# One PSUM bank for two running states, a seventh rotating bank, reordered output sessions, an earlier gate for the second weights, and last stores by halves

## The chip, the cores and the metric

The kernel runs on one NeuronCore of a Trainium2 chip, in one launch. The metric is the device time in microseconds (us) of that core. TensorE is called PE here, its weight loads PEld, VectorE is DVE, ScalarE is ACT, GpSimd is POOL, and SyncE, which issues most DMAs, is SP.

## The reference

The program is a retention layer (attention with an exponential decay in place of a softmax) followed by a two-layer network. Cut to what matters:

```python
# q, k, v: 8 batches x 8 heads x 576 positions x 64, float32
scores = q @ k.T / 8                          # per batch and head
gamma  = 1 - 2 ** (-5 - arange(8))            # one decay per head
ret    = scores * where(i >= j, gamma ** (i - j), 0)
x      = (ret @ v)                            # rearranged to 4608 tokens x 512
h      = x @ w_in                             # 512 -> 2048
g      = h * cos(h)
out    = g @ w_out                            # 2048 -> 512
```

## The kernel before

**Retention.** The decay is folded into q and v by tables of weights (`qnat`, `natv`), so that only a mask of zeros and ones is left. Work goes by units: unit (b, g) with g = 0 or 1 is positions 256g to 256g+255 of batch b; units (0, 2) and (1, 2) hold the remaining 64 positions of four batches each. Each unit's 256 positions fall into two halves, s = 0 and 1. What a later query needs of all earlier halves is the sum of k-times-v products, the running *state*: 64x64 for each head, 128x256 numbers for a batch. The state grows in PSUM (`ST`, one bank for the even batch `ST[0]` and one for the odd, `ST[1]`), and `snap` (L631) has ACT copy it to SBUF after each half.

All these matmuls are 64x64: PE is used as four quadrants, the *lanes* (row half, column half), and `emit_lanes` (L540) interleaves the instructions of the lanes. A *session* is one such run of small matmuls. A scores session (L565) makes q-k products, which DVE multiplies with the mask into `pt` (L599). An output session (`outputs`, L637) has three batches:

- main: products of `pt` and v for both halves, and the state products whose row lane is the same half's;
- states (only where there are any, `late`): the states of (u, 1) in the row lanes s = 1 and of the next unit's first half in the row lanes s = 0;
- cross: state products that run in the other half's row lanes. They add to the same banks as main, and so wait for it, by a semaphore that PE raises itself.

Two states of different batches, in two row halves of PE, thus run side by side, each into its own bank. The first state matmul of a batch clears the bank with `start=True` (L623).

**The network.** For each block j of 512 tokens (9 blocks) `mlp1` (L727) makes 16 tiles of h, four matmuls each (L737); ACT takes the cosine (L745, as a sine of h + pi/2), DVE the product into `gt` (L748). The second layer of block 0 is plain (`plain2`, L767, matmuls L776). From block 1 on it is a Strassen-Winograd product (`wino2`, L805, matmuls L862): seven products P1 to P7 in place of eight, with sums of `gt` (DVE, L823 and L829) and of the weights (`wsums`, L787, DVE L802); ACT and DVE combine them into `os`, and SP stores (`store`, L753). Products with a common sum share a PSUM bank: A, Bb and C.

**PSUM.** A partition has eight banks. Two hold the states, six rotate (`bk`): every score, output, h tile and product takes one and returns it once ACT or DVE has read it.

**The order.** It is written by a planner at build time (`Graph.run`, L204): each piece of work is a task with an engine, an estimated duration, what it reads and writes, the rotating buffers it takes, and a priority. The planner places tasks one by one on five in-order queues. It has a simple model of PE's instruction supply: every 256 instructions (`count`) a task may have to wait until 3.0 us (`FETCH`) after the last request. Where the plan has a gap on PE longer than 0.4 us, early in the kernel, `emit` (L375) puts in filler matmuls on ones (`warm`, L398). Then the list is turned into instructions with semaphores (`Prog.emit`).

**Loads.** SP loads k, q and v of each unit (0.5 MB each); POOL casts k, weights q and v. POOL also issues the weights, with a conversion to bf16: four pieces of `win` (L717) and four of `wout` (L721). The issue of `wout` waits until v of unit (1, 1) has landed; the loads of unit (2, 0) wait for the second piece of `wout` (L940 to L943):

```python
gate = [(st["v", (1, 1)], 0)]
for x in range(4):
    self.load_w("wout", x, gate, 200 + x)
self.unit((2, 0), gate=[("wout", 1, 0)])
```

Of the kernel before, what the change touches and what calls it, by code (L numbers as in the profile page):

```python
# [6 lines left out]
ALU = mybir.AluOpType  # L7
# [10 lines left out]
NTB = TOK // TB  # L18
# [111 lines left out]
class Graph:  # L130
# [3 lines left out]
    AHEAD, FETCH = 2000, 3000  # L134
# [44 lines left out]

    def first(self, t):  # L180
# [23 lines left out]
    def run(self, dma_rate):  # L204
# [3 lines left out]
        left = [256, self.FETCH]  # L208
# [21 lines left out]
        def pick(e):  # L230
            cand = []
            for t in ready[e]:
# [4 lines left out]
                if e == "pe" and t.count > left[0]:  # L237
                    s = max(s, left[1] - t.dur * left[0] / t.count)
# [22 lines left out]
        while n < len(self.tasks):  # L261
# [10 lines left out]
            e = t.eng  # L272
            ready[e].remove(t)
# [5 lines left out]
            if e == "pe":  # L279
                if t.count > left[0]:  # L280
                    left[1] = s + t.dur * left[0] / t.count + self.FETCH
                    left[0] += 256
                left[0] -= t.count
# [9 lines left out]
            if t.dma is not None:  # L293
                dma_free = max(dma_free, s + (1700 if e == "pool" else 1150)) + t.dma
                done = dma_free + t.tail
# [18 lines left out]
class Kernel:  # L314
    POOLS = dict(bk=6, stgk=3, stgv=3, stgq=3, natk=3, natv=3, qnat=2, kt=3, qt=3, pt=4, sba=3, sbb=3, sbr=8, xt=2,
# [11 lines left out]
    def __init__(self, nc, es, q, k, v, w_in, w_out, out):  # L327
# [20 lines left out]
        self.ST = [nc.alloc_psum_tensor(f"st{i}", [128, 512], F32) for i in range(2)]  # L348
# [26 lines left out]
    def emit(self, order):  # L375
# [4 lines left out]
        for t in order:  # L380
            if t.eng == "pe":
                gap = t.start - warm
                if gap > 400 and self.wb.left:
                    self.warm(int((gap - 300) / 110 if not warm else 0.6 * (gap - 150) / 57))
# [126 lines left out]
    def tpe(self, src, off, rk, dst, wk, eng):  # L511
        bk = Buf("bk")

        def mm(e):
            tb = self.at(bk).ap().bitcast(BF16)
            for c in range(4):
# [5 lines left out]
                 alloc=() if self.first else (self.wb,), name="tpe", count=9)  # L522
# [17 lines left out]
    def emit_lanes(self, name, prio, phases, alloc=()):  # L540

        parts, t, n = [], 200, 0
        for lanes, reads, writes, after in phases:
# [7 lines left out]
            n += 2 * len(order) + 1  # L551
# [60 lines left out]
    def states(self, u, s, lanes, reads, writes):  # L612
        nk, nv = self.tiles[u]["natk"], self.tiles[u]["natv"]
        x = u[0] % 2
        for r in range(2):
            for c in range(4):
                for y in range(2):
                    i, o = 512 * y + (2 * c + r) * D, 512 * y + self.head(c, r) * D
                    lanes[s, r].append((64, self.mm(
                        lambda r=r, c=c: ap(self.ST[x], 512, 64 * r, 64, c * 64, [1, 64]),  # L620
                        lambda i=i: ap(self.at(nk), 1024, 64 * s, 64, i, [1, D]),
                        lambda o=o: ap(self.at(nv), 1024, 64 * s, 64, o, [1, D]),
                        start=u[1] == s == c == y == 0)))  # L623
        reads += [(t, y) for t in (nk, nv) for y in range(2)]
        writes.append(("st", x))
# [5 lines left out]
    def snap(self, u, s):  # L631
        b = self.sbd[u, s] = Buf("sba" if s == 0 else "sbr" if u[1] else "sbb")
        x = u[0] % 2
        self.copy("act", 280, lambda: self.at(b).ap(), lambda: ap(self.ST[x], 512, 0, 128, 0, [1, 256]),
                  [("st", x)], [(b,)], late=1000 if s == 0 else 3000)

    def outputs(self, u, prio, late):  # L637
# [5 lines left out]
        main, fill, cross = ({q: [] for q in self.LANES} for _ in range(3))  # L643
# [37 lines left out]

        for s in range(2):
# [3 lines left out]
        for s in range(2):  # L686
            for p in range(2):
                inter(s, p, 1 - s, cross)
# [5 lines left out]
        phases = [(main, reads, writes, [])]  # L694
        if late:
# [305 lines left out]
```

## Time and profile before

| | us |
|---|---|
| median of three runs | 302.74 (300.94, 302.74, 304.18) |
| the profiled execution | 301.62 |
| its span, first to last instruction | 299.9 |
| PE busy | 285.2 (95% of the span) |
| DVE busy | 213.0 (71%) |
| ACT busy | 169.7 (57%) |
| POOL busy | 101.4 (34%) |
| DMA, mean rate | 166 GB/s |

A PE that is called busy is not PE at its peak, since matmuls overlap and their ends are modelled. By line, the chain that ended last is 35% L737 (first layer) and 33% L862 (second layer), then 8% loads of q, 6% L563 (small matmuls), and 3% each for the two weights. Loads of q, k and v take a median of 6.9 to 7.0 us from issue to landing, the pieces of `win` 9.0 and of `wout` 10.0, a store 3.3.

In the lines of a timeline the columns are: start in us, length in us, engine, line, operation, what it writes and reads, how many; in brackets the idle time of the engine before it and what ended that. In lists of waits: who waited for whom, us in total, how often, the longest.

### The profile page before, as it was taken

The numbers are of one execution on the slowest core, as the hardware profiler recorded it, in microseconds if no ns is written. First come the engines' busy times: TensorE is split into PE (matmuls) and PEld (weight loads), VectorE is DVE, ScalarE is ACT, GpSimd is POOL, SyncE is SP. The second block draws the span as 40 slices with busy tenths as digits, with TensorE's granted clock in tenths as the row PEclk, the third lists the DMA queues.
The fourth block names the chain that finished last, engine by engine and source line by source line (L and its number), as shares of the span: only waits on it lengthen the run. The fifth ranks groups of instructions, "written<-read, shape, count | busy, mean of one in ns | idle before, by whom it ended". The sixth has DMA issues, their size and how long they took to land.

```text
span 299.9 us, 9086 instructions
## 1 busy us (share of the span) xinstructions
PE 285.2 (95%) x3809; PEld 202.7 (68%) x3815; DVE 213.0 (71%) x379; ACT 169.7 (57%) x315; POOL 101.4 (34%) x125
## 2 busy tenths in 40 slices
PE   6789888999999999999999999999999999999994
PEld 6667665666788876766676667666766666666683
DVE  2776495659985889697868686959777666667721
ACT  5369876556667565645655565466565555545420
POOL 3821960665825614825363515172100000000000
PEclk9999999999999999999999999999999999999999
DMA  7999789999999799997999986892103000300115
GB/s 199 252 203 274 202 129 236 280 200 299 207 251 297 151 194 281 214 227 210 229 280 232 244 188 94 194 236 53 24 2 140 2 2 2 140 2 0 70 73 140
DMA packets 101640, 49.87 MB, mean 166 GB/s; under 512 B 43488, under 2 KB 97248, under 8 KB 101600
## 3 DMA queue, kind: packets, MB, share of 16 engines
q1 hardware_dynamic: 97376, 45.10, 63.6%
q0 software_dynamic: 4224, 4.19, 8.8%
q8 instruction: 30, 0.49, 0.7%
q14 instruction: 10, 0.08, 0.1%
HBM read 36.70 MB, written 9.44 MB: 154 GB/s over the span
## 4 chain that ended last, share of the span: by engine, by line
PE 78%; DMA 14%; POOL 5%; issue 1%; SPq 0%; ACT 0%; DVE 0%; DVEq 0%
PE bk L737 35%; PE bk L862 33%; DMA stgq<-in_q_dram 8%; PE bk L563 6%; DMA wout<-in_moe_w_out_dram 3%; DMA win<-in_moe_w_in_dram 3%; PE bk L776 2%; POOL qnat L496 2%; POOL natv L496 2%; PE st L563 1%; POOL natk L454 1%; SPq L463 0%; POOL win L717 0%; POOL wout L721 0%; DVE qnat L496 0%
## 5 line engine op out<-in xcount | busy, mean ns | idle before, releaser
L745 ACT ACTIVATE cb<-bk,cpi 128x256 bf16<-128x256 f32 (+1 forms) x192 | 108.3, 583 | 82.0 <-PE bk L737 79.9
L737 PE MATMUL bk<-xt,win 128*128 128x256 bf16 (+1 forms) x768 | 144.2, 326 | 1.0 <-DMA win<-in_moe_w_in_dram 0.7
L748 DVE TENSOR_TENSOR gt<-bk,cb 128x256 bf16<-128x256 f32 (+1 forms) x192 | 103.8, 555 | 54.9 <-ACT cb L745 47.8
L737 PEld LDWEIGHTS bk<-xt,win 128*128 128x128 bf16 x768 | 72.3, 98 | 39.7 <-DVE pt L599 1.4
L496 POOL TENSOR_TENSOR natv<-stgv,wv 128x512 bf16<-128x512 f32 x36 | 37.7, 1070 | 37.0 <-PE bk L563 20.6
L599 DVE TENSOR_TENSOR pt<-bk,tr 128x512 bf16<-128x512 f32 x68 | 42.7, 682 | 5.5 <-PE bk L563 5.4
L496 POOL TENSOR_TENSOR qnat<-stgq,wq 128x512 bf16<-128x512 f32 x32 | 35.0, 1112 | 15.9 <-DMA stgq<-in_q_dram 15.3
L454 POOL CAST natk<-stgk 128x512 bf16<-128x512 f32 x34 | 21.3, 653 | 55.8 <-DMA stgk<-in_k_dram 44.8
L862 PE MATMUL bk<-wout,gt 128*128 128x256 bf16 x256 | 32.7, 273 | 0.0
L862 PE MATMUL bk<-tw,s 128*128 128x256 bf16 x256 | 32.7, 273 | 0.0
L862 PE MATMUL bk<-wout,s 128*128 128x256 bf16 x256 | 32.4, 273 | 0.0
L862 PEld LDWEIGHTS bk<-tw,s 128*128 128x128 bf16 x256 | 24.9, 98 | 8.1
L862 PEld LDWEIGHTS bk<-wout,gt 128*128 128x128 bf16 x256 | 24.7, 98 | 6.4
L862 PEld LDWEIGHTS bk<-wout,s 128*128 128x128 bf16 x256 | 24.7, 98 | 6.1
L453 ACT ACTIVATE xt<-bk 128x512 bf16<-128x512 f32 x36 | 23.5, 728 | 0.5 <-PE bk L563 0.5
L874 DVE TENSOR_TENSOR os<-bk,sn 128x512 f32<-128x512 f32 x24 | 16.4, 683 | 10.4 <-PE bk L862 10.4
L453 ACT ACTIVATE sn<-bk 128x512 f32<-128x512 f32 x24 | 14.3, 597 | 13.8 <-PE bk L862 13.8
L862 PE MATMUL bk<-tw,gt 128*128 128x256 bf16 x128 | 16.4, 273 | 0.0
L776 PE MATMUL bk<-wout,gt 128*128 128x512 bf16 x58 | 15.3, 380 | 0.6 <-issue 0.3
L862 PEld LDWEIGHTS bk<-tw,gt 128*128 128x128 bf16 x128 | 12.5, 98 | 4.0
L829 DVE TENSOR_TENSOR s<-gt 128x1024 bf16<-128x1024 bf16 x16 | 12.8, 800 | 0.2
L563 PE MATMUL bk<-qt,kt 64*64 64x128 bf16 (+1 forms) x576 | 12.1, 217 | 0.4 <-ACT xt L453 0.4
(58 smaller groups left out, 187.7 us busy)
## 6 DMA issues: line engine op xcount, KB each, us to landing
stgk<-in_k_dram SPq DMA_DIRECT2D x16, 512.0 KB, 7.0
stgq<-in_q_dram SPq DMA_DIRECT2D x16, 512.0 KB, 6.9
stgv<-in_v_dram SPq DMA_DIRECT2D x16, 512.0 KB, 6.9
out_dram<-os SPq DMA_DIRECT2D x16, 512.0 KB, 3.3
win<-in_moe_w_in_dram POOLq DMA_DIRECT2D x4, 512.0 KB, 9.0
wout<-in_moe_w_out_dram POOLq DMA_DIRECT2D x4, 512.0 KB, 10.0
stgk<-in_k_dram SPq DMA_DIRECT2D x8, 128.0 KB, 3.4
stgq<-in_q_dram SPq DMA_DIRECT2D x8, 128.0 KB, 3.5
```

The lines of the kernel that those rows point to most:

```text
L453: return self.one(eng, dur, lambda e: e.activation(dst(), src(), AF.Copy), r=r, w=w, **kw)
L454: return self.one(eng, dur, lambda e: e.tensor_copy(dst(), src()), r=r, w=w, port=True, **kw)
L496: self.one(eng, 610 if eng == "dve" else 1000, lambda e, out=out, inp=inp, tab=tab, col=col, hs=hs: e.tensor_tensor(out(), inp(), ap(tab, ...
L563: return lambda e: e.matmul(out(), lhs(), rhs(), start=start, stop=True, skip_group_check=True)
L599: self.one("dve", 610, lambda e, r=r, b=b, pt=pt: e.tensor_tensor(ap(self.at(pt), 1024, 0, 128, 512 * r, [64 * ny * ny, 8 // ny // ny], [1 ...
L737: inst = e.matmul(ap(self.at(bk), 512, 0, 128, 0, [1, n]), ap(self.WIN, 4 * DFF, 0, 128, c * DFF + 128 * f, [1, 128]), ap(self.at(xt), 204 ...
L745: self.one("act", 70 + n, lambda e: e.activation(ap(self.at(cb), TB, 0, 128, 0, [1, n]), ap(self.at(bk), 512, 0, 128, 0, [1, n]), AF.Sin, ...
L748: self.one("dve", 75 + n / 0.96, lambda e: e.tensor_tensor(ap(self.at(gt), NF * TB, 0, 128, f * TB + 256 * h0, [1, n]), ap(self.at(bk), 51 ...
L776: inst = e.matmul(self.at(bk).ap(), ap(self.at(gt), NF * TB, 0, 128, f * TB + 256 * half + 128 * tt, [1, 128]), ap(self.WOUT, NF * DM, 0, ...
L829: self.one("dve", 610, lambda e, i=i, q=q, x=x, y=y, op=op: e.tensor_tensor(sv(i, q), x(), y(), op), r=r, w=[(S_[i, q],)], port=True, name ...
L862: inst = e.matmul(ap(self.at(bank), 512, 0, 128, 256 * tt, [1, 256]), l(f, tt), rr(f), start=(first and f == 0 and tt == 0), stop=True, sk ...
L874: self.one("dve", 610, lambda e: e.tensor_tensor(view(h, c), ap(self.at(bank), 512, 0, 128, 0, [256, 2], [1, 256]), ap(self.at(sn[name]), ...
```

## The change

- **State.** `ST` becomes one bank: even batch in columns 0 to 255, odd batch in 256 to 511. All states share the key `("st",)`. No state matmul clears; before the first half of each batch DVE fills its columns with zeros.
- **Banks.** `bk` goes from six to seven.
- **Output sessions.** Five batches in place of three. With row lanes 0 and 1: (cross of row half 0 | first half of the s = 1 states), (three of main | rest of these states), (rest of main | seven of main, after the first batch), (first half of the s = 0 states | rest of main, after the second), (rest of these states | cross of row half 1, after the third). Each bank is written by one row half at a time.
- **Gates.** `wout` waits for q of (1, 1) instead of v; the loads of (2, 0) wait for the third piece of `wout` instead of the second.
- **End.** In the last block, bank A becomes two banks, one for each half of the tokens; P4 runs one half after the other; copies and sums that read A are split in two; the last four stores, each of 64 partitions with 256 columns of two token tiles, become four of 128 partitions with 256 columns of one.
- **Planner.** `FETCH` 6.5 us instead of 3.0; blocks are counted from instruction 443, requested at 128, with other counts per task, and fillers are counted; a DMA from POOL that finds the engines empty is reckoned to start 0.7 us later.

```diff
-    AHEAD, FETCH = 2000, 3000
+    AHEAD, FETCH = 2000, 6500
...
-                if e == "pe" and t.count > left[0]:
-                    s = max(s, left[1] - t.dur * left[0] / t.count)
+                if e == "pe" and t.count:
+                    k = (seen + t.count - 443) // 256
+                    if k >= 0 and 443 + 256 * k > seen and k in asked:
+                        s = max(s, asked[k] + self.FETCH - t.dur * (443 + 256 * k - seen) / t.count)
...
-                if t.count > left[0]:
-                    left[1] = s + t.dur * left[0] / t.count + self.FETCH
-                    left[0] += 256
-                left[0] -= t.count
+                if gap > 400 and s < 45000:
+                    seen += 2 * self.fill(gap, seen)
+                k = (seen + t.count - 128) // 256
+                if k >= 0 and k not in asked:
+                    asked[k] = s + t.dur * max(0, 128 + 256 * k - seen) / max(1, t.count)
+                seen += t.count
...
-                dma_free = max(dma_free, s + (1700 if e == "pool" else 1150)) + t.dma
+                dma_free = max(dma_free, s + (2400 if e == "pool" and s > dma_free - 700 else 1700 if e == "pool" else 1150)) + t.dma
...
-    POOLS = dict(bk=6, stgk=3, stgv=3, stgq=3, natk=3, natv=3, qnat=2, kt=3, qt=3, pt=4, sba=3, sbb=3, sbr=8, xt=2,
+    POOLS = dict(bk=7, stgk=3, stgv=3, stgq=3, natk=3, natv=3, qnat=2, kt=3, qt=3, pt=4, sba=3, sbb=3, sbr=8, xt=2,
...
-        self.ST = [nc.alloc_psum_tensor(f"st{i}", [128, 512], F32) for i in range(2)]
+        self.ST = nc.alloc_psum_tensor("st", [128, 512], F32)
...
     def states(self, u, s, lanes, reads, writes):
+        if u[1] == s == 0:
+            self.one("dve", 340, lambda e: e.memset(ap(self.ST, 512, 0, 128, 256 * x, [1, 256]), 0.0), w=[("st",)])
...
-                        lambda r=r, c=c: ap(self.ST[x], 512, 64 * r, 64, c * 64, [1, 64]),
+                        lambda r=r, c=c: ap(self.ST, 512, 64 * r, 64, 256 * x + c * 64, [1, 64]),
...
-                        start=u[1] == s == c == y == 0)))
+                        start=False)))
-        writes.append(("st", x))
+        writes.append(("st",))
...
     def outputs(self, u, prio, late):
...
+        for p in range(2):
+            inter(1, p, 0, cross)
         for s in range(2):
             for p in range(2):
                 intra(s, p)
                 inter(s, p, s, main)
-        for s in range(2):
-            for p in range(2):
-                inter(s, p, 1 - s, cross)
+        for p in range(2):
+            inter(0, p, 1, cross)
...
-        phases = [(main, reads, writes, [])]
-        if late:
-            phases.append((fill, [], [], []))
-            for v, s in late:
-                self.states(v, s, *phases[-1][:3])
-        phases.append((cross, reads, writes, [0]))
+        state = ([], [])
+        for v, s in late:
+            self.states(v, s, late_lanes, *state)
+
+        def cut(lanes, s, i, j):
+            return {(s, p): lanes[s, p][i:j] for p in range(2)}
+
+        phases = []
+        for x, y, after in (
+                (cut(cross, 0, 0, 8), cut(late_lanes, 1, 0, 4), []),
+                (cut(main, 0, 0, 3), cut(late_lanes, 1, 4, 8), []),
+                (cut(main, 0, 3, 99), cut(main, 1, 0, 7), [0]),
+                (cut(late_lanes, 0, 0, 4), cut(main, 1, 7, 99), [1]),
+                (cut(late_lanes, 0, 4, 8), cut(cross, 1, 0, 8), [2])):
+            if any([*x.values(), *y.values()]):
+                phases.append(({**x, **y}, reads + state[0], writes + state[1], after))
...
     def store(self, j, half, os, cols=(0, DM), tts=(0, 1)):
+        if len(tts) == 1:
+            tt = tts[0]
+            self.one("sp", 640, lambda e: e.dma_start(
+                bass.AP(self.out, ((4 * half + 2 * tt) * S + 512) * DM + c0, [[S * DM, 2], [DM, 64], [1, cn]]),
+                ap(self.at(os), 1024, 0, 128, c0 + 512 * tt, [1, cn])),
+                r=reads, sem=lambda: f"o{os.slot}_{c0}_{tt}", dma=1550 * cn / DM / 2)
+            return
...
     def wino2(self, j, base, span):
-        A, Bb, C = Buf("bk"), Buf("bk"), Buf("bk")
+        last = j == NTB - 1
+        A, Bb, C = [Buf("bk") for _ in range(1 + last)], [Buf("bk")], [Buf("bk")]
...
+            halves = last and p == 4
...
-                    for f in range(4 * q, 4 * q + 4):
-                        for tt in range(2):
+                    for f in range(8) if halves else range(4 * q, 4 * q + 4):
+                        for tt in (q,) if halves else range(2):
...
-                if j == NTB - 1:
-                    self.store(j, 1, os[1], (256, 512))
-                    self.store(j, 1, os[1], (0, 256))
+                if last:
+                    for i in range(2):
+                        self.store(j, 1, os[1], (256, 512), (i,))
+                    for i in range(2):
+                        self.store(j, 1, os[1], (0, 256), (i,))
...
     def graph(self):
-        gate = [(st["v", (1, 1)], 0)]
+        gate = [(st["q", (1, 1)], 0)]
...
-        self.unit((2, 0), gate=[("wout", 1, 0)])
+        self.unit((2, 0), gate=[("wout", 2, 0)])
```

## The prediction

> **What bounds the kernel now.** I read the busy slices first, then the same engines by stage, then the waits of each stage, then single stretches of the timeline. The clock row shows that TensorE (PE) had its full clock throughout, so no edit can win or lose there.
>
> ```profile
> PE   6789888999999999999999999999999999999994
> PEclk9999999999999999999999999999999999999999
> DMA  7999789999999799997999986892103000300115
> ```
>
> By stage (start:end, length, then busy us of PE, PEld, DVE, ACT, POOL, and the clock, DMA share and GB/s):
>
> ```profile
> 17.50:28.00 10.50, 10.02 (x148) 8.40 (x149) 7.95 (x20) 8.86 (x21) 0.00 (x0) 1.00 1.21 246
> 28.00:48.50 20.50, 16.67 (x335) 12.07 (x336) 13.88 (x30) 14.93 (x35) 13.38 (x16) 1.00 0.89 180
> 48.50:62.00 13.50, 12.74 (x100) 8.30 (x100) 7.70 (x17) 7.86 (x18) 6.86 (x9) 1.00 1.12 261
> 62.00:296.00 234.00, 233.29 (x2968) 163.15 (x2968) 175.14 (x286) 128.93 (x229) 70.48 (x76) 1.00 0.65 151
> ```
>
> From 62 to 296 us PE is idle for 0.7 us of 234, and its list of waits in that stage has one entry, 0.2 us of "issue". So PE alone sets the time there: a buffer more or a load sooner is worth at most 0.7 us, and any matmul time added is paid in full. What can be won lies before 62 us, where PE waits for data, and after 295.7, where nothing but stores is left. Three stretches of the head:
>
> ```profile
> 41.11 0.45 PE L401 MATMUL bk<-one 128*128 128x128 bf16 x5
> 41.93 0.42 PE L563 MATMUL bk<-qt,kt 64*64 64x128 bf16 x16 [0.36 <-ACT xt L453]
> 43.22 0.81 PE L776 MATMUL bk<-wout,gt 128*128 128x512 bf16 x3
> 47.10 0.24 PE L563 MATMUL bk<-qt,sba 64*64 64x128 bf16 x1 [1.04 <-issue]
> 60.41 0.44 PE L563 MATMUL st<-natv,natk 64*64 64x64 bf16 x16 [0.66 <-POOL natv L496]
> ```
>
> The x5 at 41.11 are filler matmuls; PE has run out of work until the first second-layer weights arrive (L776). The 1.04 us at 47.10 sits inside one output session, between two matmuls with no wait on another engine: PE had no instructions. The DMA view of 34 to 42 us, 40 slices of 0.2 us, shows the engines empty from about 36.2 to 38.6, because the weights are issued behind a POOL multiply:
>
> ```profile
> DMA  9999879210000000000000036119599999999998
> 35.16 2.06 POOL L496 TENSOR_TENSOR qnat<-stgq,wq 128x512 bf16<-128x512 f32 x2
> 37.16 3.03 POOL L721 DMA_DIRECT2D wout<-in_moe_w_out_dram  x4
> ```
>
> **The head: second weights, bank, planner.** *Weights.* The gate moves from the landing of v(1,1) (36.38) to that of q(1,1) (34.85). POOL then casts natk(1,1) until 35.2. The weights' priority (200 to 203) is ahead of qnat's, so the four issues should go at 35.2 instead of 37.16: 2.0 us sooner, out of a 2.4 us hole. All four count: 3.03 us on POOL, behind which qnat(1,1) slips from 35.16 to 38.2; natv(1,1) still starts at 40.2, as before. The transposes and scores of (1,1) wait for qnat; they stood at 40.8 to 42.5 and can run by 41.5 to 42.5, so up to 1 us, under the first layer's matmuls. First weights land at 41.0 rather than 42.95, the last at 50.6 rather than 52.59. On SP's queue the loads of (2,0), and every later load, transpose and store behind them, now wait for the third piece: 49.52 less 2.0 is 47.5, against 47.06 now. That is no loss, since their bytes stand behind the fourth piece in either case; they land up to 2 us sooner, and the 0.66 us wait at 60.41 goes (0.8 with the switch around it). *Seventh bank.* In the head PE's matmuls also wait for banks in release (DVE gt, ACT xt, DVE pt). *Planner.* It now reckons with 6.5 us for the next instructions instead of 3.0 and counts fillers, so it should spread sessions that empty the buffer.
>
> What there is to win: 0.8 at 60.41; 1.3 around 41 to 43 (0.45 filler, 0.36, 0.18 and switches); 1.6 of missing instructions (1.04, 0.16 and what follows them); some 2.0 of the waits from 28 to 38 (qnat 1.1, banks, natk). That is 5.7. I take 0.8 + 0.9 + 0.8 + 0.5 = 3.0: half of what depends on a new order, since ACT is busy 14.9 and POOL 13.4 of 20.5 us there, and POOL's line of casts is not shortened. Bounds: 5.7 won; 1.2 lost, if the later qnat (3.0 us late, 1.8 covered) reaches PE.
>
> On missing instructions the Trainium skill, page "Runtime: NRT & Kernel Launch", section "Instruction fetch mechanics", says that fetching the next block is hidden by the issue rate. The 1.04 us row here disagrees. By the page the planner's edit would win nothing and the total below would be 0.8 us higher; the row decides.
>
> **The sessions.** Before, an output session is three batches: main, states, cross, and cross waits for main. Timeline of one (105.98 to 107.06, 1.08 us), and of a remainder session's weight loads, where no states stand between:
>
> ```profile
> 105.98 0.64 PE L563 MATMUL bk<-pt,natv 64*64 64x128 bf16 x32
> 106.57 0.42 PE L563 MATMUL st<-natv,natk 64*64 64x64 bf16 x32
> 106.82 0.24 PE L563 MATMUL bk<-qt,sba 64*64 64x128 bf16 x2
> 107.06 0.50 PE L737 MATMUL bk<-xt,win 128*128 128x256 bf16 x3
> 237.30 0.21 PEld L563 LDWEIGHTS bk<-qt,sbr 64*64 64x64 bf16 x16 [0.20 <-PE bk L563]
> ```
>
> Ten rounds of four 128-column matmuls take 106.57 - 105.98 = 0.58, so 0.056 a round (0.02 at the start). Eight rounds of states take 0.25, 0.031 a round. In the remainder session main starts at 236.64; its twelfth round starts 0.38 later, at 237.02, and cross at 237.30: a **turn** of 0.28 us from a batch's last matmul to one that waits for it. The old session hides it: main's last matmul starts at 0.53, the turn ends at 0.81, and the states end at 0.81 too. Cross then takes 0.11: 0.92, and 0.16 until the next line's matmul, 1.08.
>
> The new session has five batches; the third waits for the first, the fourth for the second, the fifth for the third. First: 0.12, last matmul at 0.09. Second: three rounds, ends 0.29. Third: may start at 0.09 + 0.28 = 0.37, so 0.08 is lost; seven rounds, last at 0.71, ends 0.76. Fourth: three rounds, 0.93 (its own wait is long over). Fifth: 0.71 + 0.28 = 0.99, so 0.06 lost; 0.12, ends 1.11. Against 0.92 that is **0.19 more**. A remainder session (rounds of 0.031; 4, 3, 9, 5 and 4 of them, the third from 0.37, the fifth from 0.90) ends at 1.03 against 0.75: 0.28 more. After 62 us there are 12 sessions and 2 remainders: 12 x 0.19 + 2 x 0.28 = 2.8 us. Behind these waits stand the session's rest and the whole dense queue of PE; ACT, which copies the result, has slack (128.9 of 234). Bounds: 0.7 if both turns vanish and only ragged batch ends stay (0.05 a session); 3.9 if each session pays one whole turn (14 x 0.28).
>
> Here the skill speaks against sharing the bank: "TensorEngine Tiling (Array Packing)", "Restrictions and Gotchas", says that different row tiles cannot access one PSUM bank at a time. No run here shows that clash. Taken alone it would run the two halves' states one after the other, 0.25 us more a session, 13 x 0.25 = 3.3; the diff instead lays them beside the other half's matmuls and pays in turns.
>
> **Zeroing.** Eight VectorE fills of 128x256. No such row; nearest are a 128x128 bf16 fill, 0.17, and a 128x256 multiply, 0.42. Each waits for ACT's copies of the state, since both halves now share one key; behind it stand DVE's masks and gt products, for which PE waits. DVE is busy 175 of 234 us and a session comes some 7 us after the copies, so 0; without that cover six in the dense stage cost 6 x 0.42 = 2.5.
>
> **The end.**
>
> ```profile
> 293.81 1.91 PE L862 MATMUL bk<-tw,gt 128*128 128x256 bf16 x16
> 295.76 0.60 ACT L453 ACTIVATE os<-bk 128x512 f32<-128x512 f32 x1 [4.64 <-PE bk L862]
> 292.99 4.70 SPq L761 DMA_DIRECT2D out_dram<-os  x6
> ```
>
> Today the last copy ends at 296.36, two stores are issued at 296.38 and 297.02, the last lands at 299.60. Now half the product is done 0.87 us earlier (8 x 0.109), copied and stored in the meantime; the last copy is 128x256, 0.40 by the state copies, and one issue follows: 295.76 + 0.40 + 0.02 = 296.18 against 297.02. Minus 0.8 us; bounds 0.2 (only the shorter copy) and 1.0.
>
> **Sum.** -3.0 + 2.8 + 0 - 0.8 = -1.0. The profiled execution took 301.62 (span 299.9), which makes 300.6. The median shown is 302.74, 1.1 above it: **301.7**.
>
> **Rivals.** *A, the turns are hidden:* sessions cost 0.7: -3.0 + 0.7 - 0.8 = -3.1, 299.6; with the whole head, 296.9. Against it stands the turn of 0.28 us, seen in both remainder sessions. *B, slower:* PE's waits on itself decide. The head's work is fixed by landings (28.3 to 36.4 us), casts and ACT, so sooner weights only move the idle time; head 0, sessions 2.8, end -0.8: +2.0, 304.7. It decides from the point where the head gives under 2.0 us. With the delayed qnat too (1.2), 305.9. For it speaks that POOL's line is no shorter. *C, the seventh bank does what it is for in the middle:* at most 0.7 us, 301.0; PE does not wait for banks there.
>
> **Numbers.** Forecast 0.50, A 0.22, B 0.26, C 0.02. One per cent is 3.0 us, about what a measurement of this kernel can tell from no change. Faster by over that: A's and a tail of the forecast, 0.24. Slower: over half of B, 0.16. Within: 0.60. Range: down to the forecast with half of A's two terms, 298.0; up to B with the late qnat, 306.0. The forecast's own, with the head 1.5 either way, is 300.2 to 303.2.
>
> **What would show it.** Right: output sessions of 1.25 to 1.30 us instead of 1.05 to 1.08, with PEld waits on "PE bk"; weights issued near 35.2; no "issue" wait of 1 us before 50; the last store issued some 0.5 us after the last matmul's end (295.72 before) instead of 1.3. Wrong: sessions under 1.15 us; PE idle in the middle; or the first L776 matmul not before 43.

## The result, and the profile after

| | before | after |
|---|---|---|
| median, us | 302.48 (300.94 to 304.18) | 312.74 (312.5 to 314.37) |
| profiled execution, us | 301.62 | 314.37 |
| its span | 299.9 | 312.6 |
| last matmul ends | 295.73 | 298.94 |
| from there to the end | 4.18 | 13.71 |
| mean output session after 62 us, instruction waits left out | 1.07 | 1.29 |

The changed kernel is slower by 3.5% (ratio 1.0349, 95% interval 1.0283 to 1.0416); 301.7 had been forecast, and at most 306.0. Three rows of the page of after, 40 slices each; in PE's row the idle end is now a slice and a half long, and the clock fell early on:

```profile
PE   7769999999999999999999999999999999999920
PEclk9997999999999999999999999999999999999995
DMA  7999899999999199989999987821030003003041
```

The end, from the timeline (start, length, engine, line, operation, count):

```profile
295.94 1.28 SPq L780 DMA_DIRECT2D out_dram<-os  x2
297.03 1.91 PE L896 MATMUL bk<-tw,gt 128*128 128x256 bf16 x16
297.95 1.31 SPq L791 DMA_DIRECT2D out_dram<-os  x2
298.98 0.38 ACT L462 ACTIVATE os<-bk 128x256 f32<-128x256 f32 x1 [0.49 <-PE bk L896]
299.30 4.11 SPq L780 DMA_DIRECT2D out_dram<-os  x2
```

The last copy does end at 299.36, 0.4 us after the last matmul, as forecast. But the last two stores keep SP's queue for 4.11 us instead of 1.3, and the DMA view of 296 to 313 us (40 slices of 0.43 us, busy share of 16 engines in tenths, then the rate) shows how slowly they move. Below it stands the same view of the kernel before, 290 to 302 us in slices of 0.3 us:

```profile
DMA  0001101115969889971110011111111111100000
GB/s 0 0 10 29 39 27 31 34 48 72 96 92 145 116 164 217 342 275 48 48 14 7 24 29 29 41 48 48 48 51 48 46 48 51 41 24 24 14 0 0
```

```profile
DMA  0000000100000049796189999986994000000000
GB/s 0 0 0 0 0 0 0 27 0 0 0 0 0 0 119 205 181 222 147 27 198 212 218 164 246 341 225 160 304 362 164 0 0 0 0 0 0 0 0 0
```

From 304 us on the engines of after are a tenth busy, at 51 GB/s or less and mostly 48. The stores of line L791, in the old form, pass in the middle at up to 342 GB/s; the four new ones (L780, 128 KB each) crawl before and after them.

The sessions came as forecast. Parts of the session that starts at 104.15; its third batch starts at 104.54, its fourth at 104.84, its last at 105.20, and the next line's matmul at 105.44:

```profile
104.15 0.24 PE L572 MATMUL bk<-qt,sba 64*64 64x128 bf16 x2
...
104.54 0.47 PE L572 MATMUL bk<-pt,natv 64*64 64x128 bf16 x20
104.84 0.22 PE L572 MATMUL bk<-qt,sbb 64*64 64x128 bf16 x2
...
105.21 0.24 PE L572 MATMUL bk<-qt,sbb 64*64 64x128 bf16 x2
...
105.44 0.39 PE L896 MATMUL bk<-wout,s 128*128 128x256 bf16 x2
```

In the head the weights were issued at 34.95, and the wait for instructions near 47 us is gone. But a longer one has come up much earlier, within the output session that starts at 19.74, and the clock falls after it (windows: start:end, length, busy us of PE, PEld, DVE, ACT, POOL, granted clock, DMA share, GB/s):

```profile
23.33 0.24 PE L572 MATMUL bk<-qt,sba 64*64 64x128 bf16 x2 [2.50 <-issue]
34.95 3.04 POOL L743 DMA_DIRECT2D wout<-in_moe_w_out_dram  x4 [0.37 <-DMA stgq<-in_q_dram]
```

```profile
22.00:24.00 2.00, 0.67 (x5) 0.48 (x6) 0.00 (x0) 0.38 (x1) 0.00 (x0) 0.87 1.24 209
24.00:26.00 2.00, 2.00 (x11) 1.43 (x10) 0.36 (x1) 1.91 (x5) 0.00 (x0) 0.50 1.14 313
26.00:28.00 2.00, 2.00 (x16) 1.59 (x14) 0.86 (x3) 0.93 (x3) 0.41 (x1) 0.77 1.20 299
```

### The profile page after: what moved, and what is told of

It reads as the page before. It is cut to its first block, busy times and chain, and to the rows that moved or that the text cites. A ratio compares the mean times of both kernels' runs of the same rounds, so it can differ in the third digit from the quotient of the medians.

```text
span 312.6 us, 9105 instructions
## 1 busy us (share of the span) xinstructions
PE 289.7 (93%) x3800; PEld 206.8 (66%) x3806; DVE 214.5 (69%) x388; ACT 169.2 (54%) x318; POOL 101.8 (33%) x125
## 3 DMA queue, kind: packets, MB, share of 16 engines
q0 software_dynamic: 4224, 4.19, 8.7%
## 4 chain that ended last, share of the span: by engine, by line
PE 86%; DMA 4%; DVE 2%; issue 2%; ACT 1%; POOL 1%; SPq 0%; DVEq 0%; ACTq 0%
PE bk L759 40%; PE bk L896 31%; PE bk L572 8%; PE bk L805 4%; DMA win<-in_moe_w_in_dram 2%; DMA stgq<-in_q_dram 2%; PE st L572 2%; PE bk L526 1%; POOL natv L505 1%; DVE gt L770 1%; DVE s L858 0%; DVE s L852 0%; DVE pt L608 0%; ACT cb L767 0%; DVE qnat L505 0%
## 5 line engine op out<-in xcount | busy, mean ns | idle before, releaser
L759 PE MATMUL bk<-xt,win 128*128 128x256 bf16 (+1 forms) x768 | 147.9, 329 | 0.8 <-DMA win<-in_moe_w_in_dram 0.4
L759 PEld LDWEIGHTS bk<-xt,win 128*128 128x128 bf16 x768 | 73.1, 99 | 36.8 <-ACT sbb L462 0.5
L505 POOL TENSOR_TENSOR qnat<-stgq,wq 128x512 bf16<-128x512 f32 x32 | 35.3, 1126 | 9.4 <-DMA stgq<-in_q_dram 9.4
L896 PEld LDWEIGHTS bk<-tw,s 128*128 128x128 bf16 x256 | 24.9, 98 | 8.1
L896 PEld LDWEIGHTS bk<-wout,gt 128*128 128x128 bf16 x256 | 24.9, 98 | 7.2 <-DVE pt L608 0.3
L916 DVE TENSOR_TENSOR os<-bk,sn 128x512 f32<-128x512 f32 (+1 forms) x25 | 16.5, 662 | 14.4 <-PE bk L896 14.4
L462 ACT ACTIVATE sn<-bk 128x512 f32<-128x512 f32 (+1 forms) x26 | 14.5, 566 | 9.0 <-PE bk L896 9.0
L572 PE MATMUL st<-natv,natk 64*64 64x64 bf16 x512 | 15.6, 195 | 1.0 <-POOL natv L505 0.7
L572 PE MATMUL bk<-pt,natv 64*64 64x128 bf16 (+1 forms) x576 | 15.8, 217 | 0.0
```

Of the source, the lines that this page charges most:

```text
L462: return self.one(eng, dur, lambda e: e.activation(dst(), src(), AF.Copy), r=r, w=w, **kw)
L505: self.one(eng, 610 if eng == "dve" else 1000, lambda e, out=out, inp=inp, tab=tab, col=col, hs=hs: e.tensor_tensor(out(), inp(), ap(tab, ...
L572: return lambda e: e.matmul(out(), lhs(), rhs(), start=start, stop=True, skip_group_check=True)
L759: inst = e.matmul(ap(self.at(bk), 512, 0, 128, 0, [1, n]), ap(self.WIN, 4 * DFF, 0, 128, c * DFF + 128 * f, [1, 128]), ap(self.at(xt), 204 ...
L896: inst = e.matmul(place(bank, tt), l(f, tt), rr(f), stop=True, skip_group_check=True, start=(first and f == 0 and tt < len(bank)))
L916: self.one("dve", 610 // len(bank), lambda e, i=i, b=b: e.tensor_tensor(view(h, c, i, len(bank)), flat(self.at(b), 0, len(bank)), flat(sel ...
```

## The experiments

The theory after this profile, called W in the expectations: the form of the last stores' address in DRAM is the loss. It begins with a dimension of size 2, and a store so written uses two of the 16 DMA engines. The main rival: a store of 128 partitions that crosses from one batch of the output to the next is slow in itself. Besides, the head and the sessions had to be priced one by one. Medians below come with those of the kernel before on the same chip (301.7 to 302.1). The ratio beside them is measured separately and is not their quotient: the two differ by up to 1.4 us, so a difference of about 1 us between two runs is not told from none.

### The end

**The end alone, in the kernel before** (`store`, `plain2` and `wino2` of after, nothing else).

> Kernel before, with the changed end alone (two banks for A in the last block, P4 by halves, the four stores in their changed form); sessions, banks, gates and planner as before. Theory W: the last matmul at 295.7 us as before, the end after it 13 to 14 us instead of 4.2: slower by 8.5 to 10 us, 311 to 312.5. If instead the lateness of the sessions or of the head is what makes the stores collide, this one has no loss: 302.

Measured: 312.28 us against 302.05, ratio 1.0312 (1.0236 to 1.0388); 13.58 us from the last matmul to the end. The end alone makes nearly all of the loss. Its profile, the slowest of its four executions, has one thing more that is not the end's and that was not expected: the last matmul comes 3.2 us later than before, after 1.83 us without instructions near 47 us and a clock of 0.50 from 50 to 52 us.

**Each new store as two of 64 rows**, in after:

```diff
-  [[S * DM, 2], [DM, 64], [1, cn]]   <- 128 partitions
+  [[DM, 64], [1, cn]]                <- 64 partitions, twice
```

> Changed kernel, but each of the four last stores (two batches x 64 rows x 256 columns, 128 KB) is issued as two stores of 64 rows. Theory W (the store whose outermost output dimension has size 2 is carried by two DMA engines; 512 KB at the 48 GB/s seen at the end take 10 us): the last matmul stays where it was, the end after it falls from 13.7 us to some 4, and the time falls by 8.5 to 10 us to 303-304. Rival S (many small stores at the end are slow, whatever their form): eight stores of 64 KB in place of four are no better, 312 or more. Rival Q (these stores wait behind the two 256 KB stores of the first half): no change, 312.

Measured: 305.28 against 302.05, ratio 1.006 (1.0022 to 1.0097), end 5.53 us. The slow stretch is gone, so the number of stores (rival S) and the two larger ones ahead of them (rival Q) are not what made it. SP now issues ten stores, each 0.6 us, and these rows bind the end (last matmul 296.99):

```profile
293.98 2.47 SPq L781 DMA_DIRECT2D out_dram<-os  x4
296.49 1.30 SPq L792 DMA_DIRECT2D out_dram<-os  x2
297.83 2.93 SPq L781 DMA_DIRECT2D out_dram<-os  x4
```

This run cannot tell W from its rival, since it changes the dimension and the partitions at once. A first attempt to tell them apart failed by its own design: **64 rows as two blocks of 32**, `[[32 * DM, 2], [DM, 32], [1, cn]]`.

> The 64-row stores of the run with ten short stores, each with its 64 rows of DRAM described as two blocks of 32 (the first dimension of the address has size 2). Same bytes, same ten issues, same SBUF side. Theory W (the first dimension of the DRAM address decides how many of the 16 DMA engines carry a store, and 2 leaves two of them): the eight stores of 64 KB, 512 KB in all, go at some 50 GB/s again, so the end after the last matmul is 9 to 13 us and the time 308 to 313 us. Rival (what cost time in the changed kernel was that one store covers 128 partitions, or that a store crosses from one batch of the output to the next): the end stays at 5.5 us and the time at 304 to 306.

Measured: end 5.52 us, 306.46 us. That looks like the rival's win, but 32 steps of one row are one step of 32 rows: the two dimensions describe one of 64, and the run says nothing if they were joined on the way (which was not read from the instruction). So two more, which cannot be joined: **64 rows as 2 by 32**, `[[DM, 2], [2 * DM, 32], [1, cn]]`, and **64 rows as 32 by 2**, `[[DM, 32], [32 * DM, 2], [1, cn]]`:

> The run with ten short stores once more, each store's 64 rows of DRAM now described as 2 by 32 with the 2 taking neighbouring rows (steps of one row, then of two rows), so that the two dimensions cannot be joined into one of 64, as the blocks of 32 in the earlier run could. The rows of these blocks land in another order than the reference's. Theory W (the size of the first DRAM dimension sets how many engines carry a store): eight stores at 50 GB/s together, 512 KB in some 10 us, so an end of 9 to 13 us and 308 to 313 us. Rival (what was slow is a store of 128 partitions that crosses from one batch of the output to the next): end 5.5 us, 304 to 307 us.

> The same with the rows as 32 by 2 (steps of 32 rows, then of one), again not to be joined, again in another row order. Theory W: the first dimension is 32, all engines carry it, end 5.5 us, 304 to 307 us. Rival (two dimensions that cannot be joined are slow whatever their sizes): the same 9 to 13 us as with 2 by 32.

Measured, one execution each: 2 by 32, an end of 13.34 us and 316.92 us; 32 by 2, an end of 5.57 us and 304.84 us. Of the 12.1 us between them 7.8 are the end; 4.3 come before the last matmul, in the first run, whose clock was 0.50 from 24 to 30 us. The DMA views, of the first from 299 to 316 us and of the second from 294 to 304:

```profile
DMA  0001111112596999621111001111111111000000
GB/s 0 0 10 12 43 31 41 31 22 58 96 159 116 217 234 316 217 84 48 53 53 27 24 29 48 51 46 48 48 51 46 48 48 48 27 24 14 0 0 0
```

```profile
DMA  0000000551814608239798999879246073000000
GB/s 0 0 0 0 0 0 0 147 115 29 205 29 111 152 16 197 49 98 254 172 238 147 213 287 344 254 275 283 58 106 152 4 188 74 0 0 0 0 0 0
```

Same bytes, same issues, same 64 partitions: only which dimension stands first differs, and with it the order of the rows. The step between rows does not sort slow from fast: it is one row both in after (slow) and in the ten short stores (fast). W is shown, its engines too: from 304 to 311 us of after and from 308 to 313 us of the run with 2 by 32 the DMA share is 0.13, and 0.13 of 16 is 2.1 engines. The rate of 48 GB/s is the same in both: 24 GB/s for each of two engines, at which 512 KB take 10.9 us. The Trainium skill, page "DMA: Bandwidth & Descriptors", section "Why a DMA increments its semaphore by 16 and not by 1", has the rule: the engines used are the largest number up to 16 that divides the slowest dimension other than 1 of both addresses. These two runs agree with it.

**After with the whole end of before** (everything else of the change stays).

> The changed kernel with the whole end of the kernel before (last product in one bank, its stores in two whole-block parts); head, planner, seven banks and new sessions stay. Theory (the end is the whole loss; sessions cost 3 us and the head gives 1 to 3 back, and the 2.5 us without instructions at 23 us is already in that sum): end 4.2 us after the last matmul, time 302 to 304.5 us, that is the changed kernel's 312.7 less 9.4. Rival (the changed end also cost time before the last matmul): last matmul's end before 296 and time near 300.6, as forecast without the end's 0.8. Rival (sessions cost more than their own length): 305 or more.

Measured: 303.89 against 301.9, ratio 1.004 (1.0002 to 1.0079), end 4.19 us. By the ratios the end is 1.0349 - 1.004 = 3.1%, some 9.3 us, as by the profiles (13.71 - 4.19 = 9.5). What is left of the change is a loss of about 1.2 us by the ratio (interval 0.1 to 2.4), 2.0 by the medians.

**The end as it was meant, in the kernel before**: halves, the early column half stored as before, the last four stores of 64 rows issued by SP and ACT in turn.

```diff
-  self.one("sp", 640, lambda e, i=i: e.dma_start(
+  self.one("act" if i else "sp", 640, lambda e, i=i: e.dma_start(
```

> The kernel before with the end as the change meant it and no store with a dimension of 2: last product by halves into two banks, the column half that is ready early stored as before (two stores), the last column half by four 64-row stores, two issued by SP and two by ACT right behind ACT's own copies. Theory: the last copy ends 0.40 us after the last matmul instead of 0.63, its two stores are issued side by side instead of 0.64 us after each other and carry 64 KB (2.0 us to landing instead of 2.6): end 2.6 to 3.2 us instead of 4.18, time 1.0 to 1.6 us less than the kernel before, ratio 0.995 to 0.997. Rival (an issue on ACT costs ACT as much as on SP, and delays the second copy by 0.6 us): end 3.2 to 3.8. Rival (the changed graph of the end shifts the planner's order before): last matmul moves by over 1 us either way and hides the gain.

Measured: 302.69 against 301.7, ratio 1.0027 (0.9988 to 1.0066); end 4.39 us, no shorter than 4.18. The miss has three parts. ACT's own issue holds up its second copy by 0.2 us. SP issues the last store at 298.13, 0.6 us after that copy, since the store ahead of it (297.20) keeps its queue for 0.9 us. And the last four stores take a median of 2.9 us (ACT's) and 3.2 us (SP's) to land instead of 2.0. Timeline of the end (last matmul 296.90), then the windows in which the last stores land, of this run and of before:

```profile
296.48 0.59 ACTq L759 DMA_DIRECT2D out_dram<-os  x1
297.12 0.39 ACT L453 ACTIVATE os<-bk 128x256 f32<-128x256 f32 x1 [0.67 <-PE bk L875]
297.20 2.01 SPq L759 DMA_DIRECT2D out_dram<-os  x2
297.53 0.48 ACTq L759 DMA_DIRECT2D out_dram<-os  x1
```

```profile
298.00:300.00 2.00, 0.00 (x0) 0.00 (x0) 0.00 (x0) 0.00 (x0) 0.00 (x0) 1.00 0.93 248
```

```profile
296.00:298.00 2.00, 0.00 (x0) 0.00 (x0) 0.00 (x0) 0.36 (x1) 0.00 (x0) 1.00 0.97 235
```

The engines are 0.93 and 0.97 busy in these windows. The last block's whole output, 1 MB in both kernels, is issued within 4 to 5 us, and at 235 to 248 GB/s it takes 4.2 to 4.5 us alone. So an earlier copy of the last quarter joins a queue that is nearly full. How much of the miss is that and how much SP's late issue, this run does not separate.

### The sessions

**Old sessions, two state banks, six rotating banks**, in the run with the ten short stores.

> As e1, but with two state banks, six rotating banks and the output sessions of before (three batches); gates, planner and end by halves stay. Theory T (PE's waits on itself in the five-batch sessions cost 0.22 us a session): output sessions back to 1.05-1.08 us, remainder sessions to 0.91, and 3 us less than e1: 300 to 301. Rival B7 (the seventh bank gives back what the sessions cost): no difference to e1, or slower by up to 1 us. Rival H (the loss in the middle comes from the plan, not from the sessions): no difference to e1.

Measured: 304.13 us against 302.05, ratio 1.004 (1.000 to 1.0079), sessions 1.085 us again: 1.1 us less than with the new ones by the medians and 0.6 by the ratios, not clear of noise, where 3 were expected. The sessions' own saving is there in the trace (12 sessions 15.49 us long in the run with ten short stores, 12.78 before; two remainders 1.15 against 0.91: 3.2 us), but the order around them loses 1.1 us of it in waits for DVE that the run with ten short stores does not have, and the seventh bank is gone with the new sessions; the two are not separated here:

```profile
PE bk L884 <- DVE gt L757: 0.6, 1, 0.6
PE bk L746 <- DVE gt L757: 0.3, 1, 0.3
PE bk L746 <- DVE pt L608: 0.2, 1, 0.2
```

### The head

To compare heads, the matmuls that PE has started by a given time are added up, each with its length at the full clock (0.109 us for 128x256, 0.216 for 128x512, and so on; fillers count nothing; matmuls missing from a trace, six at most, are put back). This *useful work*, in us:

| by | before | old end | 9 us for one block | old gate |
|---|---|---|---|---|
| 28 us | 12.4 | 10.5 | 11.9 | 10.5 |
| 48 us | 25.2 | 27.4 | 24.9 | 26.7 |
| 60 us | 36.7 | 37.9 | 35.3 | 38.4 |
| 85 us | 59.2 | 61.2 | 58.1 | 58.7 |
| 290 us | 257.0 | 256.3 | 253.0 | 252.3 |

The columns are the kernel before, after with the whole end of before, and that run with one more edit each; the edits follow. In the profile of the third one the clock fell to 0.50 from 48 to 50 us (0.65 from 46 to 48), which takes some 1.7 us off its rows from 60 us on; it stayed up in the others.

**The gates alone, in the kernel before.**

```diff
-        gate = [(st["v", (1, 1)], 0)]
+        gate = [(st["q", (1, 1)], 0)]
...
-        self.unit((2, 0), gate=[("wout", 1, 0)])
+        self.unit((2, 0), gate=[("wout", 2, 0)])
```

> Kernel before with the two gates moved, nothing else. If the sooner second weights are worth what I forecast for them (0.8 at the wait for natv and 0.9 around the first second-layer matmul): 1.0 to 2.0 us faster than before, 300.7 to 301.7, second weights landing some 2 us sooner. If the head's work is fixed by landings, casts and ACT: same time within 0.5 us.

Measured: 302.78 against 302.05, ratio 1.0003 (0.996 to 1.0047). The weights land sooner, the first second-layer matmul starts at 41.25 instead of 43.22, and nothing is left of it: waits of 0.67 (ACT, at 41.25), 0.48 (the next weights, at 48.01) and 0.62 (DVE, at 83.8) take the time back.

**The old planner**, in after with the old end.

> The changed kernel with the whole old end and with the old planner (3.0 us for the next block of instructions, fillers not counted); new sessions, seven banks and the gate stay. Theory (the wait of 2.3 us at 23 us comes of the new session order, which lets PE use up its instructions 1.9 us sooner, and not of the planner): the wait stays at 2 to 2.5 us, a second wait of 0.5 to 2 us comes back near 45 us, time 303.5 to 306 us. Rival (the new planner put the session there): no wait over 1 us before 30 us, time 301 to 303 us.

Measured: 304.63 against 301.7, ratio 1.0066 (1.0025 to 1.0106). The wait before 24 us stays; the one near 45 us does not come back. So the new wait comes not of the planner but of the new session order. PE's instructions come in blocks (the instruction queue moved 30 of 16 KB in after), and one of them is late there: in the kernel before and with the old sessions, where PE waits 0.2 to 0.3 us there, PE first needs that block at 22.4 us, with the new ones at 20.3 to 20.7. From the list of waits, 10 to 62 us (who waits for whom, total, times, longest):

```profile
PE bk L754 <- issue: 3.1, 2, 2.8
```

**10 us from request to instructions instead of 6.5 for every block, and 9 us for the one block that came late**, both in after with the old end.

> As the run with the old end, but the planner reckons with 10 us from the request for the next block of instructions to its arrival instead of 6.5. Theory (the 2.5 us at 23 us is a block that came 8.7 us after its request while the planner reckoned with 6.5, and the session could have been put later): the wait at 23 us goes or falls under 1 us, other work takes its place, and the time is 1 to 2.5 us under the run with the old end. Rival (nothing else is ready for PE there, the first-layer weights have not landed): fillers or waits for data take the place, the time is within 0.5 us of it.

> The changed kernel with the whole old end; the planner reckons with 9 us instead of 6.5 for one block of instructions alone, the one that came 8.7 to 8.8 us after its request and for which PE waited 2.3 to 2.5 us. That moves the output session near 20 us behind sixteen first-layer matmuls (16 x 0.11 = 1.8 us) and seven fillers. Theory (that wait is what eats the head, once as lost time and once more in the runs whose clock falls after it): no wait for instructions over 0.8 us before 30 us, the granted clock stays at 1.00 from 22 to 28 us in every profile, 0.5 to 1.8 us more useful work by 28 us, time 0.5 to 3 us under the run with the old end and its 303.9. Rival (the planner's order after it is another one and loses the same in other waits, as with 10 us for every block): the wait goes, the time stays within 1 us of 303.9 or is longer, and the waits between 40 and 90 us say where.

Measured: 308.56 us (1.0207, 1.0142 to 1.0272) and 304.67 us (1.0055, 1.0017 to 1.0093). In both the wait near 23 us goes (none; 0.6 us) and the clock stays at 1.00 from 22 to 28 us. With 9 us, 1.4 us more work is done by 28 us, as the theory had it; by 48 us it is 2.5 us less, because PE, further on, runs into a copy that is not done and weights that have not landed, and the clock falls after that (0.7 of the 2.5 us by 48 us). From its timeline:

```profile
41.42 1.02 PE L798 MATMUL bk<-wout,gt 128*128 128x512 bf16 x4 [0.83 <-ACT qt L462]
...
46.31 1.63 PE L798 MATMUL bk<-wout,gt 128*128 128x512 bf16 x4 [1.51 <-DMA wout<-in_moe_w_out_dram]
```

The rival is right: the wait for instructions was a place where PE waited, not what set the time of the head. The clock's fall in the profile does not make this result: nine of the ten executions with 9 us had a mean clock of 0.997 or more, and they took 303.7 to 305.1 us.

**The gates undone**, in after with the old end.

> The changed kernel with the whole old end and the second weights issued at the old place, behind the multiply of qnat(1,1) near 37 us instead of 35 us. Theory (the sooner weights are worth something in the changed order, since PE has nothing else near 41 us): first second-layer matmul 1 to 2 us later than the 42.9 of the run with the old end, 0.5 to 1.5 us less useful work at 51 us, time 0.5 to 1.5 us longer. Rival (no value, as in the kernel before with the sooner weights alone): useful work at 75 us within 0.3 us, time within 0.7 us.

Measured: 306.23 against 301.96, ratio 1.0131 (1.0096 to 1.0165): 2.3 us more than with the new gates, and by neither account. The first second-layer matmul comes at 45.65 instead of 42.85, yet at 60 us more work is done, not less. The loss comes between 60 and 85 us, and at 160:

```profile
69.56 1.87 DVE L608 TENSOR_TENSOR pt<-bk,tr 128x512 bf16<-128x512 f32 x3
70.30 1.21 PE L759 MATMUL bk<-xt,win 128*128 128x256 bf16 x8 [1.01 <-DVE pt L608]
77.13 0.42 PE L572 MATMUL bk<-qt,kt 64*64 64x128 bf16 x16 [0.74 <-DVE pt L608]
160.23 1.02 PE L759 MATMUL bk<-xt,win 128*128 128x512 bf16 x4 [1.05 <-DVE gt L770]
```

DVE has the sums of block 1's gt and of the weights to make there, and in two windows of 5 us it is busy throughout, PE not (with the new gates DVE is as busy in them, 5.00 and 4.99, but PE has 4.84 and 5.00, so a full DVE alone does not make the loss; the order of its work counts too):

```profile
70.00:75.00 5.00, 4.70 (x109) 3.18 (x110) 5.00 (x11) 2.25 (x5) 2.74 (x4) 1.00 1.14 328
75.00:80.00 5.00, 4.08 (x45) 2.91 (x46) 5.00 (x10) 2.96 (x9) 4.75 (x6) 1.00 1.22 247
```

**Six banks instead of seven**, in after with the old end.

> As the run with the old end, but with six rotating banks: the seventh, freed by putting both states into one bank, stays unused. Theory (the seventh bank matters in the head alone): PE waits for banks in release between 28 and 50 us grow by 0.3 to 1 us, nothing changes after 62 us, time 0 to 1 us longer. Rival (banks do not bind the head either): the same within 0.3 us in the work done by 60 us. Rival (the seventh bank let PE run ahead into the instruction wait at 23 us): that wait falls under 1 us and the time is 1 us shorter.

Measured: 307.48 against 301.9, ratio 1.0188 (1.0108 to 1.0268): 3.6 us more than with seven, more than any account had. In its profile the clock fell to 0.50 from 24 to 26 us and in that of the old end it did not, which is some 1.7 us between these two profiles. The largest new wait is again one for DVE:

```profile
84.58 1.07 DVE L770 TENSOR_TENSOR gt<-bk,cb 128x256 bf16<-128x256 f32 x3
85.14 1.03 PE L884 MATMUL bk<-wout,gt 128*128 128x256 bf16 x8 [1.06 <-DVE gt L770]
```

Each of these edits also makes the planner write another order. How much of 2.3 or 3.6 us belongs to the gate or the bank as such, and how much to the order that happened to come out, these runs do not separate. No version beat the kernel before: the gates alone and the end on two queues are nearest, both within their intervals of it.

## Why the prediction was wrong, step by step

**The end (-0.8): the step that failed, by 10 us.** It counted copies and issues and took a store's time from issue to landing as given. The diff showed the new address, `[[S * DM, 2], [DM, 64], [1, cn]]`, and it was read for bytes and partitions only. Measured: +9.5 us. In its place the runs showed two of 16 engines at 48 GB/s: the size of the address's first dimension set the time of the end. Nor was the term right for a store in a good form: the gain by halves is 0 (4.39 against 4.18 us), with the DMA engines nearly full and SP's queue late. The full engines could be read from the profile before: 0.97 busy from 296 to 298 us.

**The sessions (+2.8): the turns and their size right, what they cost not shown.** 3.2 us measured in the sessions' own rows; undoing them, with the bank, gave 0.6 to 1.1 us of time, so that "any matmul time added is paid in full" did not show. The third batch starts 0.39 us after the first (forecast 0.37), the last 1.05 (0.99), the whole takes 1.285 to 1.30 (1.25 to 1.30). One sign was wrong: no row names PE as what its weight loads wait for in these sessions.

**The head (-3.0): it gave less, and its parts did not hold.** From the profiles, with all that is neither session nor end put down to the head: with the old end the last matmul ends 0.7 us later than before, sessions cost 3.4 in that run, so the rest gave 2.7; in the run with ten short stores 1.3 and 3.2, so 1.9; in after the sessions' rows add up to 3.8 (two hold waits for instructions) and the last matmul is 3.2 later, so 0.6, and the clock accounts for 1.6 of the difference. By times instead of profiles, with the old end: 3.4 less the loss of 1.2 to 2.0, so 1.4 to 2.2. "No edit can win or lose" by the clock, read from the profile before, was wrong too: in after it fell to 0.50. The terms:

- *The missing instructions (0.8):* 1.04 us at 47 us went, 2.50 at 23 came. Which session needs a block, and when, was never worked out for the new session order. The prediction's quarrel with the page "Runtime: NRT & Kernel Launch" stands: 2.50 us here is not hidden.
- *Around the first second-layer matmul (0.9):* issued at 34.95, at 35.2 in the forecast, and the weights landed 1.2 to 2.3 us sooner; but that matmul came at 44.41 in after, so the sign named as wrong showed. Alone the gates gave nothing.
- *The seventh bank:* given part of 0.5 us in the head and, as rival C, at most 0.7. Without it the changed kernel takes 3.6 us more, order and clock included.
- *"PE alone sets the time" after 62 us:* true of the profile before, and wrong as a rule for another order. DVE was 175 of 234 us busy on average, but 9.96 of 10 from 70 to 80. In the run with the old gate PE came there 0.5 us ahead of the run with the old end and waited; in that one it did not.

**Rival B**, slower by the head's giving under 2.0 us, is half right. Without the end's term the forecast's sum is -0.2 us and B's +2.8; after with the old end lost 1.2 to 2.0, between the two. B's reason, that sooner work only moves the idle time, is borne out by the runs with gates alone and with 9 us: sooner work met weights and DVE. No rival had the store.

**Zeroing (0): no cost shows.** A fill takes 0.27 us. In after no matmul waits for one; one weight load does, between 10 and 20 us (1.4 us), and DVE once stands idle for 2.6 us, between 90 and 110 us, until ACT has copied the state. Behind that, PE's list of waits shows nothing over 0.4 us. No run leaves the fills out.

## What to carry to other kernels

Read the address of every store that a diff touches: which dimension stands first, on both sides, and its size (here 2 was slow where it could not be joined with the next dimension; 32, 64 and 128 were not); a bad one cost 9.5 us where a gain of 0.8 had been forecast. A shorter tail of compute may be worth nothing where the last stores already fill the DMA engines, as here, so look at their busy share after the last matmul first. Where a planner writes the order, look for the next stretch in which another engine is fully busy, in windows of 5 us and not over the whole stage: that is where a lead may be lost.

## What the runs showed of the hardware

- Two DMA engines (a share of 0.13 of 16) carried 48 GB/s, and the issue of two such stores held SP's queue for 4.11 us instead of 1.3.
- A block of instructions that PE had come to the request point of sooner arrived later. The instruction queue's packets came from 19.66 to 20.60 us in the profile before and from 20.91 to 21.84 in after; the point at which PE reached instruction 384, where the request is supposed to go out (an inference from all blocks of these traces), is 14.19 and 13.10. The DMA engines were full of first-layer weights in both.
- After the same idle time of 2.5 us the clock fell in some executions and not in others; with 9 us for one block it fell after 1.51 us. The run with ten short stores and the one with blocks of 32 have the same order and the same wait; 24 to 28 us in their windows:

```profile
24.00:26.00 2.00, 2.00 (x21) 1.80 (x19) 0.35 (x1) 2.00 (x6) 0.00 (x0) 1.00 1.15 324
26.00:28.00 2.00, 2.00 (x20) 1.65 (x19) 2.00 (x7) 2.00 (x6) 0.56 (x2) 1.00 1.20 294
```

```profile
24.00:26.00 2.00, 2.00 (x13) 1.48 (x11) 0.36 (x1) 2.00 (x6) 0.00 (x0) 0.55 1.15 316
26.00:28.00 2.00, 2.00 (x13) 1.47 (x12) 0.84 (x4) 0.74 (x2) 0.52 (x1) 0.60 1.20 296
```

By 28 us the first has done 10.53 us of useful work and the second 8.89: a fallen clock costs 1.6 us here, and the last matmul ends at 296.99 and 299.22.
